# Two S4 and SwiGLU layers on one core: the convolution kernel's stage laid out by a table of times, its spread sent through DRAM, and its tail rewritten

## The chip, the cores and the metric

The kernel runs on one core of a Trainium2 chip. The metric is the device time in microseconds (us) of one launch. The engines are TensorE (PE in the profile; PEld is its weight load), VectorE (DVE), ScalarE (ACT), GpSimd (POOL) and SyncE (SP, which here only issues DMAs). Each engine works through its own list of instructions in order and waits on semaphores; DMAs are issued from SP's list and from POOL's.

## The reference, cut to what matters

```python
def _A_ref(u, ...):                       # S4 convolution, 512 channels, 128 states, L = 2048
    dt = jnp.exp(log_dt)[:, None]
    P = jnp.exp((dt * A)[:, :, None] * l)                 # channel, state, lag
    K = jnp.einsum("dn,dnl,dn->dl", C, P, dt * B).real    # the kernel of the convolution
    y = causal_convolution(u, K)                          # written there with FFTs of 4096
    return y + u * Dskip

def _B_ref(x, w_gate, w_up, w_down):      # 512 -> 1376 -> 512
    return (silu(x @ w_gate) * (x @ w_up)) @ w_down

for layer in range(2):                    # x is 2048 x 512, the same weights in both layers
    x = x + _A_ref(layernorm(x), ...)
    x = x + _B_ref(layernorm(x), ...)
```

## The kernel before, in words

Time is cut into 4 blocks of 512 rows, the channels into 8 **chunks** of 64 (`NCH`). There are four stretches.

**Start.** Inputs and tables are loaded, `dt` is formed, the factors of chunk 0 are made, and the spectra of the first input block are taken (`direct`, PE).

**Kernel stage.** One turn of a loop for each chunk i, with `K` as the product of two factors: lag = 64 b + a. Factor `g` (32 values of b, real and imaginary, 64 channels) is grown by doubling: `gen_g` (DVE) multiplies the n values it has by z^n and appends them, for n = 1, 2, 4, 8, 16. Factor `re`, `im` (64 values of a) is a cosine or sine times an exponential: `gen_turns` multiplies the angle by its table (DVE), `gen_reduce` takes off whole turns (ACT, DVE), `gen_trig` and `gen_exp` look up sine and exponentials (ACT), and `gen_e` multiplies them (DVE); `mu` holds the exponentials of the upper half. `lags` makes K with 128 small matmuls into `pk`, ACT copies it to `ks`, and `spread` moves it from rows of channel groups to rows of lags with 16 matmuls against the identity and 4 for `Dskip` (`kp`, copied to `kt`). `spectra` takes the spectra of the four blocks of K with 32 f32 matmuls of 256 columns (`pw`, four frequency groups q); ACT copies each to `s1`, POOL copies the first block into `w0r` (L503) and makes the sums of neighbouring blocks (L509), and SP stores them to `wdr` in DRAM. In a turn i, the matmuls `lags(i)` stand beside the factors of chunk i+1 and the tables of chunk i+2. Two more jobs are spread over the turns: `norms` (sums of squares of the feed-forward weights: loads by SP, squares by ACT, matmuls against ones, a maximum by DVE; they give the scales of the f16 split) and `second` (spectra of the second input block, one q a turn).

**Tail.** The last two chunks' spectra, the convolution of block 0 in layer 0 (`ssm(0, 0)`: products on DVE, inverse transform `pi` on PE), the norm of its first 256 rows, and the beginning of the split of the weights into an f16 high and low part.

**Feed-forward stretch.** For the eight pairs of layer and block: three f16 matmuls for each weight tile (high by high, high by low, low by high, L806 to L808), SiLU and product (L811 to L814), `py` (L820 to L822), with the convolution of the next pair between them.

In the first three stretches the lists of ACT, DVE and PE are in the order of the code (`manual_schedule`). That order is written out by hand with generators: `take(gg, 1)` emits the next piece of a generator. SP's and POOL's lists, and everything in the feed-forward stretch, are put in order by the scheduler. PSUM is two buffers of 4 KB a partition (`big`: `pk`, `kp`, `pgu`, `py`) and four of 2 KB (`sml`). The pieces of the code on which the change turns:

```python
def stats(...):   # G is GpSimd, V is VectorE
    G.tensor_scalar(rs[:, :rows], mv[:, :rows, 1], EPS, 1.0 / scale ** 2, OP.add, OP.mult)
    G.tensor_tensor(rs[:, :rows], rs[:, :rows], mhalf[:, :rows], OP.pow)
    G.tensor_tensor(nb[:, :rows], mv[:, :rows, 0], rs[:, :rows], OP.mult)
    G.tensor_scalar(nb[:, :rows], nb[:, :rows], -1.0, None, OP.mult)
# spectra, for each q after the copy of pw to s1:
    G.tensor_copy(w0r[:, h, q, :, off:off + DC]..., s1[:, :, 0])          # L503
    for i in range(2):
        G.tensor_tensor(wo[:, i], s1[:, i, 1:], s1[:, 1 - i, :3], ops[i])   # L509
# gen_g, the last doubling, twice 8 values of b:
    V.tensor_tensor(tmp, g[:, ::-1, b0:b0 + step], zi..., OP.mult)          # L441
    V.tensor_tensor(g[:, 0, o], g[:, 0, o], tmp[:, 0], OP.subtract)         # L444
    V.tensor_tensor(g[:, 1, o], g[:, 1, o], tmp[:, 1], OP.add)              # L445
```

Of the kernel before, what the change touches and what calls it, by code (L numbers as in the profile page):

```python
# [40 lines left out]
INV = 1  # L41
SEQ = ((0, 0), (0, 1), (0, 2), (1, 0), (0, 3), (1, 1), (1, 2), (1, 3))
# [30 lines left out]
def kernel(ctx, tc, x, a_re, a_im, b_re, b_im, c_re, c_im, log_dt, d_skip,  # L73
# [9 lines left out]
    BUFS = dict(W0=1, W1=1, W2=1, W3=1, ga=1, gb=1, n=1, bt=1, z=1, u=2, y1=1, uu=3, w=3, t=1, bb=2, dd=2, t1=3,  # L83
                xf=1, nn=1, hh=1, hl=1, sg=2, hf=1, stats=2, stats2=2, ef=1)
# [29 lines left out]
    cr, ci = load(c_re, "cr", "sg"), load(c_im, "ci", "sg")  # L114
# [20 lines left out]
    ones = tl([P, P], "ones", "dd")  # L135
    G.memset(ones, 1.0)
    onesb = sb.tile([P, P], BF16, name="onesb")
    G.memset(onesb, 1.0)
    hpi = sb.tile([P, 1], F32, name="hpi")
# [4 lines left out]
    xdr = dram.tile([NB, 4, P, D], F32, name="xdr")  # L144
    ndr = dram.tile([2, 2, P, 2, HD], F32, name="ndr")
# [34 lines left out]
    nc.sync.dma_start(dsk, d_skip)  # L180


    def stats(src, rows, scale, tag="stats", between=None):
# [10 lines left out]
        G.tensor_scalar(rs[:, :rows], mv[:, :rows, 1], EPS, 1.0 / scale ** 2, OP.add, OP.mult)  # L194
        G.tensor_tensor(rs[:, :rows], rs[:, :rows], mhalf[:, :rows], OP.pow)
        G.tensor_tensor(nb[:, :rows], mv[:, :rows, 0], rs[:, :rows], OP.mult)
        G.tensor_scalar(nb[:, :rows], nb[:, :rows], -1.0, None, OP.mult)
# [84 lines left out]
    def second(h, q, space=psml):  # L282
        n = []
        for cp in range(2):
            t = tl([P, 2, HD], "n1", "w")
            nc.sync.dma_start(t, ndr[h, cp])
            n += [t[:, 0], t[:, 1]]
        return direct(1, h, q, n, space)


    def norms():
# [7 lines left out]
        for gi, group in enumerate(groups):  # L299
            acc = psml([P, group[0][1].shape[1]], "nrm")  # L300
            for k, (wi, src) in enumerate(group):
                rows, cols = src.shape
                st = tl([P, cols], "st", "w")
                nc.sync.dma_start(st[:rows], src)
                sq = tl([P, cols], "sq", "t1", BF16)
                A.activation(sq[:rows], st[:rows], AF.Square)
                last = k == len(group) - 1

                def product(acc=acc, sq=sq, rows=rows, k=k, last=last):
                    PE.matmul(acc, lhsT=onesb[:rows], rhs=sq[:rows], start=k == 0, stop=last)  # L310
# [3 lines left out]
                yield product, largest if last else None  # L314
# [24 lines left out]
    def gen_tiles(ch):  # L339
# [3 lines left out]
        xz = tl([P, 5, DC], "xr", "bb"), tl([P, 5, DC], "xi", "dd")  # L343
# [4 lines left out]
    def gen_turns(ch, ts):  # L348

        re, im, mu, xz, mz, t16 = ts  # L350
        t_ = th[:, ch * DC:(ch + 1) * DC]
        V.tensor_tensor(t16, am[:, 5:].unsqueeze(2).to_broadcast([P, 16, DC]), bd(t_, 16), OP.mult)
        yield
        V.tensor_tensor(xz[1], am[:, :5].unsqueeze(2).to_broadcast([P, 5, DC]), bd(t_, 5), OP.mult)
        G.memset(im[:, 32], 0.0)
        yield

    def gen_reduce(ts):
# [3 lines left out]
        A.activation(xz[0].bitcast(I32), xz[1], AF.Copy)  # L362
# [8 lines left out]
        V.tensor_tensor(xz[1], xz[1], xz[0].bitcast(I32), OP.subtract)  # L371
# [14 lines left out]
    def gen_exp(ch, ts):  # L386

        re, im, mu, xz, mz, t16 = ts
# [5 lines left out]
        for a0, o in ((0, re), (32, mu)):  # L394
            for a in [a for a in range(a0 + 1, a0 + 33) if a < 64 and (a % 2 or a % 8 == 0)]:
                A.activation(o[:, a - a0], r_, AF.Exp, scale=32.0 * a)
                yield
            for st in (2, 4):
                A.activation(o[:, st:33:2 * st] if a0 == 0 else o[:, st::2 * st],
                             re[:, (a0 + st) // 2:(a0 + 34) // 2:st], AF.Square)  # L400
                yield

    def gen_e(ts):


        half = [[t.rearrange("p a (g h d) -> p a g h d", g=4, h=2)[:, :, :, o] for t in ts[:3]] for o in range(2)]
# [6 lines left out]
        for re, im, mu in half:  # L413
            V.tensor_tensor(re[:, 33:64], re[:, 33:64], mu[:, 1:], OP.mult)
            yield
            V.scalar_tensor_tensor(im[:, 33:64], im[:, 33:64], -1.0, mu[:, 1:], OP.mult, OP.mult)
            yield

    def gen_g(ch, ts, g):
# [12 lines left out]
        for n in (1, 2, 4, 8, 16):  # L432
            yield
            lv = n.bit_length() - 1
            zr, zi = (t[:, lv:lv + 1, :].unsqueeze(1) for t in xz)
            V.tensor_tensor(g[:, :, n:2 * n], g[:, :, 0:n], zr.to_broadcast([P, 2, n, DC]), OP.mult)
            step = min(n, 8)
            for b0 in range(0, n, step):
                tmp = tl([P, 2, 8, DC], "tmp", "bt")[:, :, :step]
                o = slice(n + b0, n + b0 + step)  # L440
                V.tensor_tensor(tmp, g[:, ::-1, b0:b0 + step], zi.to_broadcast([P, 2, step, DC]), OP.mult)  # L441
                if b0 + step == n:
                    yield
                V.tensor_tensor(g[:, 0, o], g[:, 0, o], tmp[:, 0], OP.subtract)  # L444
                V.tensor_tensor(g[:, 1, o], g[:, 1, o], tmp[:, 1], OP.add)  # L445
        yield

    def lags(ts, g):
        re, im = ts[:2]
        pk = pbig([P, 16, 64], "pk")  # L450
        for d in range(DC):
            grp, dd = d % 4, d // 4
            d = 16 * grp + dd
# [391 lines left out]
    with tc.manual_schedule(engines={mybir.EngineType.Activation, mybir.EngineType.DVE, mybir.EngineType.PE}):  # L845
# [171 lines left out]
        while tops:  # L1017
            tops.pop(0)()
# [76 lines left out]
```

## Time and profile before

| | |
|---|---|
| device time, median of 3 runs | 1219.86 us (1213.67 to 1221.53) |
| device time of the profiled execution | 1211.11 us |
| span of the profiled execution | 1209.3 us |
| start (to the first `lags`) | 54.3 us |
| kernel stage, `lags` of chunk 0 to `lags` of chunk 7 | 235.6 us |
| tail, `lags` of chunk 7 to the first feed-forward matmul | 59.7 us |
| feed-forward stretch | 859.7 us |
| busy PE, DVE, ACT, POOL | 1129.1, 1041.4, 632.1, 191.7 us |

The stretches are the stages of one profiled execution, cut where `lags` begins (54.3, 289.9) and where the first matmul of the feed-forward stretch begins (349.6). "Busy" is the time in which an engine had an instruction running. A row of the timeline has its start, its length, the engine, line and operation, output and inputs, the size, how many are merged in it, and in brackets the idle time before it and what ended it. Instructions overlap a little, so the step from one start to the next is shorter than the length shown. One f32 matmul of the code stands as two MATMUL rows.

### The profile page before, as it was taken

How to read it: one execution, taken by the hardware profiler on the slowest of the kernel's cores; microseconds unless marked ns; L12 is line 12 of the kernel's file. 1: busy time of each engine (PE TensorE's matmuls, PEld its weight loads, DVE VectorE, ACT ScalarE, POOL GpSimd, SP SyncE). 2: the span in 40 equal slices, each digit the busy share in tenths (PEclk: the TensorE clock that was granted, in tenths of full speed). 3: DMA queues.
4: the chain of work that ended last, by engine and by line, in shares of the span. 5: the costliest groups of instructions: out<-in, count | busy, mean ns of one | idle time of the engine just before them, and what ended most of it. 6: DMA issues, size and time to landing. Idle time of an engine off the chain costs nothing.

```text
span 1209.3 us, 25387 instructions
## 1 busy us (share of the span) xinstructions
PE 1129.1 (93%) x10220; PEld 887.6 (73%) x10220; DVE 1041.4 (86%) x1685; ACT 632.1 (52%) x1392; POOL 191.7 (16%) x209
## 2 busy tenths in 40 slices
PE   3989999979988998989999999999999999999998
PEld 2867878767876686858686877777686776867875
DVE  7999999988769999899999999999993799983221
ACT  6998888852256445536754623564432553324111
POOL 1024437653130010101100000120000010000000
PEclk9999999989999999999999999999999999999999
DMA  6223322236389425632245453334434144311000
GB/s 227 105 86 89 86 72 70 83 94 179 108 258 312 123 71 169 160 118 90 69 135 148 128 169 133 110 96 146 141 118 138 37 116 132 117 58 44 14 23 18
DMA packets 134857, 138.66 MB, mean 115 GB/s; under 512 B 75921, under 2 KB 85137, under 8 KB 134738
## 3 DMA queue, kind: packets, MB, share of 16 engines
q1 hardware_dynamic: 132178, 128.64, 35.4%
q0 software_dynamic: 2560, 8.39, 2.0%
q8 instruction: 80, 1.31, 0.5%
q14 instruction: 39, 0.32, 0.1%
HBM read 98.71 MB, written 28.31 MB: 105 GB/s over the span
## 4 chain that ended last, share of the span: by engine, by line
PE 34%; DVE 25%; issue 5%; DMA 3%; ACT 2%; POOL 2%; SPq 1%; DVEq 0%; ACTq 0%; POOLq 0%
PE pgu L806 6%; PE pgu L807 6%; PE pgu L808 6%; DVE t L682 4%; PE py L820 4%; PE py L821 3%; PE py L822 3%; DVE yk L685 3%; PE pi L701 3%; PE pf L260 2%; DVE yk L682 2%; DVE z L216 2%; POOL rs L211 2%; DMA mix<-nn 2%; DVE sg L812 1%
## 5 line engine op out<-in xcount | busy, mean ns | idle before, releaser
L806 PE MATMUL pgu<-mix,wsl 128*128 128x256 f16 x1280 | 349.6, 273 | 6.4 <-DVE sg L812 3.8
L808 PE MATMUL pgu<-mix,wsl 128*128 128x256 f16 x1280 | 349.7, 273 | 1.3 <-DVE wsl L578 1.3
L807 PE MATMUL pgu<-mix,wsl 128*128 128x256 f16 x1280 | 349.7, 273 | 0.0
L807 PEld LDWEIGHTS <-wsl 128*128 128x128 f16 x1280 | 125.5, 98 | 22.9 <-issue 7.2
L820 PE MATMUL py<-wsl,hh 128*128 128x512 f16 (+1 forms) x352 | 134.5, 382 | 7.6 <-DVE xg L825 3.5
L808 PEld LDWEIGHTS <-wsl 128*128 128x128 f16 x1280 | 125.5, 98 | 16.6 <-DVE wsl L578 1.6
L806 PEld LDWEIGHTS <-wsl 128*128 128x128 f16 x1280 | 125.5, 98 | 15.7
L822 PE MATMUL py<-wsl,hl 128*128 128x512 f16 (+1 forms) x352 | 134.4, 382 | 2.4 <-DVE hl L814 2.4
L811 ACT ACTIVATE sg<-pgu,sc 128x512 f32<-128x512 f32 x80 | 54.6, 682 | 132.0 <-PE pgu L808 114.1
L682 DVE TENSOR_TENSOR t<-uu,w 128x1024 f32<-128x1024 f32 x96 | 118.1, 1230 | 5.6 <-DMA uu<-udr 5.4
L821 PE MATMUL py<-wsl,hh 128*128 128x512 f16 x320 | 122.1, 382 | 0.0
L685 DVE TENSOR_TENSOR yk<-yk,t 128x1024 f32<-128x1024 f32 x96 | 118.0, 1229 | 0.2
L812 DVE SCALAR_TENSOR_TENSOR sg<-pgu,sc,sg 128x512 f32<-128x512 f32 x80 | 60.4, 756 | 52.2 <-ACT sg L811 52.0
L492 PE MATMUL pw<-kt,ek 128*128 128x256 f32 (+2 forms) x420 | 103.1, 386 | 0.0
L701 PE MATMUL pi<-yl,mix 128*128 128x256 f16 x672 | 91.4, 272 | 4.1 <-ACT yl L690 3.5
L492 PEld LDWEIGHTS pw<-kt,ek 128*128 128x128 f32 x420 | 81.9, 203 | 10.9
L813 ACT ACTIVATE hh<-sg 128x512 f16<-128x512 f32 x80 | 50.0, 625 | 57.8 <-DVE sg L812 57.7
L503 POOL COPY w0r<-s 128x128 f32<-128x128 f32 x29 | 58.5, 2016 | 127.1 <-ACT s L501 98.4
L211 POOL TENSOR_TENSOR rs<-mv,mhalf 128x2 f32<-128x2 f32 (+1 forms) x21 | 36.5, 1740 | 263.8 <-ACT mv L210 248.3
L260 PE MATMUL pf<-z,eh 128*128 128x256 f16 x576 | 74.6, 273 | 1.3 <-ACT z L250 1.3
L701 PEld LDWEIGHTS <-mix 128*128 128x128 f16 x672 | 65.3, 98 | 13.3 <-issue 2.4
L682 DVE TENSOR_TENSOR yk<-u,w0r 128x1024 f32<-128x1024 f32 x56 | 68.7, 1227 | 0.3 <-ACT u L262 0.3
(221 smaller groups left out, 2336.3 us busy)
## 6 DMA issues: line engine op xcount, KB each, us to landing
w<-wdr SPq DMA_DIRECT2D x96, 256.0 KB, 2.8
uu<-udr SPq DMA_DIRECT2D x96, 256.0 KB, 3.0
udr<-u POOLq DMA_DIRECT2D x32, 256.0 KB, 2.7
wdr<-wo SPq DMA_DIRECT2D x96, 64.0 KB, 2.0
udr<-u SPq DMA_DIRECT2D x16, 256.0 KB, 2.5
n<-ndr SPq DMA_DIRECT2D x16, 256.0 KB, 2.9
n<-xdr SPq DMA_DIRECT2D x4, 1024.0 KB, 5.5
xg<-in_A_u_dram SPq DMA_DIRECT2D x3, 1024.0 KB, 6.1
```

Of the source, the lines that this page charges most:

```text
L260: PE.matmul(pf[:, o], lhsT=e, rhs=m, start=k == 0, stop=k == len(terms) - 1)
L492: PE.matmul(pw[:, i], lhsT=e, rhs=kt[:, :, c + 4 * k0:4 * k1:4, :].rearrange("p g k d -> p k g d"), start=c == 0, stop=c == 3)
L682: V.tensor_tensor(t, uu.unsqueeze(1).to_broadcast([P, 2, 2, HD]), w.unsqueeze(2).to_broadcast([P, 2, 2, HD]), OP.mult)
L685: V.tensor_tensor(yk, yk, t, OP.add)
L701: PE.matmul(pi[:, o], lhsT=e, rhs=m, start=k == 0, stop=k == len(terms) - 1)
L806: PE.matmul(o, lhsT=wgu(wi, k, 0)[:, fs], rhs=nh[:, k], start=k == 0, stop=False)
L807: PE.matmul(o, lhsT=wgu(wi, k, 0)[:, fs], rhs=nlo[:, k], start=False, stop=False)
L808: PE.matmul(o, lhsT=wgu(wi, k, 1)[:, fs], rhs=nh[:, k], start=False, stop=k == 3)
L812: V.scalar_tensor_tensor(sg, pgu[:, 1], sc6[:, 4:5], sg, OP.mult, OP.mult)
L820: PE.matmul(py[:, r], lhsT=hh[:n, f, rc], rhs=wd(f, 0)[:n], start=f == 0, stop=False)
L821: PE.matmul(py[:, r], lhsT=hh[:n, f, rc], rhs=wd(f, 1)[:n], start=False, stop=False)
L822: PE.matmul(py[:, r], lhsT=hl[:n, f, rc], rhs=wd(f, 0)[:n], start=False, stop=f == FT - 1)
```

## The change

- **Order.** The turns of the kernel stage and the tail are no longer written as a sequence of `take`. Every piece is entered in a list with a time (`at(t, piece)`), the list is sorted, and the pieces are emitted in that order. SP's list in this stretch is in the order of the code now. The times only set the order.
- **g.** The subtraction and the addition of a doubling become one addition for both parts, with the negative sine made by ACT (`xz[:, 2]`). The last doubling of chunks 1 to 7 makes its second product in one instruction, and a DMA from POOL's queue adds it to `g` (`accum_op=OP.add`).
- **mu.** The upper half's exponentials are squares of the lower half's: one ACT instruction (`upper`) for 19 exponentials and 2 squares. For chunks 6 and 7 the angles are made by ACT in 21 small instructions, not by DVE.
- **Spread.** For chunks 0 to 5 `kt` is made by a DMA to DRAM (`kdr`) and four back. Chunks 6 and 7 use the identity matmuls. `Dskip` is added in `products` by a matmul of one row.
- **Spectra.** Two q at a time into one `big` buffer; ACT makes the signed copy from PSUM and `w0r`, DVE adds (L552 of the new code), and SP stores with one DMA for each q.
- **norms.** The loads go to POOL's queue, and loads, squares, products and maxima have times of their own.
- **stats.** The small operations around the power go from POOL to DVE.
- **Tail.** `spectra_parts` in place of `spectra`; the convolution is cut into two halves (`ssm_half`) whose pieces have times; the norm of the first rows is a generator (`first_norm`); the split of the weights uses other buffers in another order.
- **Feed-forward stretch.** The four low-by-high matmuls come after the eight others of a group; one tile `sg2` with two halves replaces two buffers of `sg`.

```diff
 def stats(src, rows, scale, tag="stats", between=None, then=None):
...
-    G.tensor_scalar(rs[:, :rows], mv[:, :rows, 1], EPS, 1.0 / scale ** 2, OP.add, OP.mult)
+    V.tensor_scalar(rs[:, :rows], mv[:, :rows, 1], EPS, 1.0 / scale ** 2, OP.add, OP.mult)
     G.tensor_tensor(rs[:, :rows], rs[:, :rows], mhalf[:, :rows], OP.pow)
-    G.tensor_tensor(nb[:, :rows], mv[:, :rows, 0], rs[:, :rows], OP.mult)
-    G.tensor_scalar(nb[:, :rows], nb[:, :rows], -1.0, None, OP.mult)
+    if then:
+        then()
+    V.scalar_tensor_tensor(nb[:, :rows], mv[:, :rows, 0], -1.0, rs[:, :rows], OP.mult, OP.mult)
...
+def upper(ts):
+    A.activation(ts[2][:, 1:], ts[0][:, 1:32], AF.Square)
...
+        if n == 16 and ch:
+            tmp = tl([P, 2, 16, DC], "acc", ("gb", "ga")[ch % 2] if ch < NCH - 1 else "W0")
+            V.tensor_tensor(tmp, g[:, ::-1, 0:16], xz[:, 2:0:-1, lv:lv + 1].to_broadcast([P, 2, 16, DC]), OP.mult)
+            G.dma_start(g[:, :, 16:32].rearrange("p i b d -> p i (b d)"), tmp.rearrange("p i b d -> p i (b d)"),
+                        accum_op=OP.add)
+            continue
...
+def spread(ch, ks, kt, eng=nc.sync):
+    k = kdr[ch % 2]
...
+    eng.dma_start(k.rearrange("g b a f -> (g b) a f"), ks.rearrange("p a c d -> p a (c d)"))
+    for ga in range(4):
+        eng.dma_start(kt[32 * ga:32 * ga + 32].rearrange("p g c d -> p g (c d)"), k[:, :, ga].rearrange("g b f -> b g f"))
...
+def spectra(ch, kt, q0):
...
+    pw = pbig([P, 2, 2, NB, 4, 16], "pw")
+    for j in range(2):
+        products(ch, pw[:, j], kt, 0, NB, q0 + 2 * j, [(i, c) for i in range(2) for c in range(4)])
+    yield
...
+    for i, sign in signs(q0):
+        A.activation(wv[:, :, i], pv[:, :, 1 - i, :3 * DC], AF.Copy, scale=sign)
+    A.activation(w0r[:, h, q0::2, :, off:off + DC], wf[:, :, :, 0], AF.Copy)
+    yield
+    V.tensor_tensor(wv, pv[:, :, :, DC:], wv, OP.add)
+    yield
+    for j in range(2):
+        store_w(h, off, q0 + 2 * j, wo[:, j])
...
+    def use(c, t):
...
+        at(t, lambda: box.update(pk=lags(ts[c], gs[c])))
+        at(t + 7.1, copy)
...
+    starts = [0.0, 31.0, 62.0] + [93.0 + 28.0 * k for k in range(NCH)]
+    for i in range(NCH - 1):
+        t = starts[i]
+        use(i, t)
+        factors(i + 1, t)
+        second_block(i, t)
+        if i + 2 < NCH:
+            prepare(i + 2, t)
...
                     for k in range(4):
                         PE.matmul(o, lhsT=wgu(wi, k, 0)[:, fs], rhs=nh[:, k], start=k == 0, stop=False)
-                        PE.matmul(o, lhsT=wgu(wi, k, 0)[:, fs], rhs=nlo[:, k], start=False, stop=False)
-                        PE.matmul(o, lhsT=wgu(wi, k, 1)[:, fs], rhs=nh[:, k], start=False, stop=k == 3)
+                        PE.matmul(o, lhsT=wgu(wi, k, 1)[:, fs], rhs=nh[:, k], start=False, stop=False)
+                    for k in range(4):
+                        PE.matmul(o, lhsT=wgu(wi, k, 0)[:, fs], rhs=nlo[:, k], start=False, stop=k == 3)
```

Three places of the engines' lists follow. First DVE's list from the last doubling of `g` to the start of the next turn, in a turn of the kernel stage. `acc` and `tmp` hold the second product, `spare` and `wo` are the sums for `wdr`. Before:

```order
L436 TENSOR_TENSOR g<-g,xr 128x2x1024
L441 TENSOR_TENSOR tmp<-g,xi 128x1024
L444 TENSOR_TENSOR g<-g,tmp 128x512
L445 TENSOR_TENSOR g<-g,tmp 128x512
L441 TENSOR_TENSOR tmp<-g,xi 128x1024
L414 TENSOR_TENSOR re<-re,mu 128x124x8
L416 SCALAR_TENSOR_TENSOR im<-im,mu 128x124x8
L444 TENSOR_TENSOR g<-g,tmp 128x512
L445 TENSOR_TENSOR g<-g,tmp 128x512
```

And now:

```order
L469 TENSOR_TENSOR g<-g,xz 128x2x1024
L472 TENSOR_TENSOR acc<-g,xz 128x2048
L552 TENSOR_TENSOR spare<-pw,spare 128x768
L393 TENSOR_TENSOR xz<-xz 128x320
L396 SCALAR_TENSOR_TENSOR im<-t_1237,re 128x1024
L396 SCALAR_TENSOR_TENSOR im<-t_1237,re 128x512
L396 SCALAR_TENSOR_TENSOR im<-t_1237,re 128x256
L396 SCALAR_TENSOR_TENSOR im<-t_1237,re 128x128
L396 SCALAR_TENSOR_TENSOR im<-t_1237,re 128x64 x2
L443 TENSOR_TENSOR re<-re 128x32x32 x2
L446 TENSOR_TENSOR re<-re,mu 128x31x32
L448 SCALAR_TENSOR_TENSOR im<-im,mu 128x31x32
```

The four additions of 512 are gone, a sum over 768 elements of `pw` has come in behind `acc`, and the taking off of whole turns (L393, L396), which stood between the doublings, now follows it. Second, POOL's list in one turn of the kernel stage (`s` is the copy of `pw`; the two memsets belong to the tables of a later chunk). Before:

```order
L503 COPY w0r<-s_1021 128x2x64
L509 TENSOR_TENSOR wo<-s_1021 128x192 x2
L393 MEMSET re 128x64
L355 MEMSET im 128x64
L503 COPY w0r<-s_1095 128x2x64
L509 TENSOR_TENSOR wo<-s_1095 128x192 x2
```

And now:

```order
L473 DMA g<-acc 128x2x1024
L418 MEMSET re 128x64
L377 MEMSET im 128x64
L316 DMA st<-in_B_w_gate_dram 128x344 x3
L473 DMA g<-acc 128x2x1024
```

POOL's arithmetic on `s` is gone from the stage; the adding DMA and the loads of weights have taken its place. Third, DVE's list in the start, at the mean and variance of the first input block (`mv`, `rs`). Before:

```order
L192 BN_STATS st<-xne 128x6
L193 BN_AGGR mv<-st 128x2
L371 TENSOR_TENSOR xi<-xi,xr 128x320
L374 SCALAR_TENSOR_TENSOR im<-t_163,re 128x1024
L374 SCALAR_TENSOR_TENSOR im<-t_163,re 128x512
```

And now:

```order
L203 BN_STATS st<-xne 128x6
L204 BN_AGGR mv<-st 128x2
L205 TENSOR_SCALAR rs<-mv 128x4
L209 SCALAR_TENSOR_TENSOR rs<-mv,rs 128x4
L393 TENSOR_TENSOR xz<-xz 128x320
L396 SCALAR_TENSOR_TENSOR im<-t_166,re 128x1024
```

Two small instructions have come in; the second reads what POOL's power makes of the first's result, and the rest of DVE's list stands behind it. The same pair stands again behind the statistics of the second block.

More of the change, by code (lines that the diff above doesn't have):

```diff
@@ L134 @@
     G.memset(epst[:, 1:2], EPS / 256.0 ** 2)
[L135 removed]
+    ones = tl([P, P], "ones", "bd")
     G.memset(ones, 1.0)
@@ L138 @@
     G.memset(onesb, 1.0)
+    one = sb.tile([P, 1], F32, name="one")
+    G.memset(one, 1.0)
     hpi = sb.tile([P, 1], F32, name="hpi")
```

641 lines of the change are left out of this document (345 added, 296 removed).

## The prediction, made before the result was known

> **What bounds the kernel now.** I read the busy shares of the stages first, cut at DVE's turns of the kernel stage and at the starts of `lags`. The columns are length, then busy PE, PEld, DVE, ACT, POOL with counts, then granted clock and DMA.
>
> ```profile
> 58.87:89.68 30.81, 26.84 (x310) 21.00 (x304) 30.74 (x48) 29.98 (x89) 6.49 (x8) 0.94 0.29 90
> 89.68:123.39 33.71, 32.30 (x383) 25.72 (x375) 33.64 (x49) 30.57 (x88) 16.26 (x15) 0.95 0.32 87
> ...
> 220.80:261.70 40.90, 32.65 (x383) 26.18 (x382) 37.32 (x57) 30.57 (x91) 25.52 (x17) 0.87 0.29 77
> 261.70:289.90 28.20, 26.80 (x372) 21.99 (x372) 26.58 (x32) 10.68 (x28) 13.10 (x10) 1.00 0.50 147
> 289.90:349.60 59.70, 55.94 (x531) 49.52 (x531) 45.01 (x89) 18.82 (x30) 18.47 (x28) 0.97 0.54 160
> 349.60:1209.30 859.70, 825.29 (x6913) 636.12 (x6911) 719.11 (x1176) 378.26 (x717) 57.99 (x70) 0.99 0.38 115
> ```
>
> A turn is DVE's: 33.64 busy in 33.71 us. The first turn, with 6.5 us of POOL instead of 16, is 2.9 us shorter for nearly the same list. The tail and the feed-forward stretch are PE's (55.9 of 59.7; 825 of 860). In the stage 220.80 to 261.70 all engines idle; the waits name a late load of weights:
>
> ```profile
> ACT sq L306 <- DMA st<-in_B_w_up_dram: 7.1, 1, 7.1
> ```
>
> Next, whether DVE's work is slow or much. Equal instructions in the start (rows 1, 3) and in the stage (rows 2, 4), where POOL's copies and sums run, mean ns after the comma:
>
> ```profile
> L416 DVE SCALAR_TENSOR_TENSOR im<-im,mu 128x992 f32<-128x992 f32 x2 | 2.4, 1189 | 0.0
> L416 DVE SCALAR_TENSOR_TENSOR im<-im,mu 128x992 f32<-128x992 f32 x10 | 13.9, 1387 | 0.0
> ...
> L352 DVE TENSOR_TENSOR t<-am,th 128x1024 f32<-128x1024 f32 x1 | 1.2, 1222 | 0.0
> L352 DVE TENSOR_TENSOR t<-am,th 128x1024 f32<-128x1024 f32 x5 | 8.0, 1599 | 0.0
> ...
> L503 POOL COPY w0r<-s 128x128 f32<-128x128 f32 x17 | 33.8, 1988 | 63.1 <-ACT s L501 34.4 <-DMA st<-in_B_w_gate_dram 28.6
> L509 POOL TENSOR_TENSOR wo<-s 128x192 f32<-128x192 f32 x32 | 31.6, 1007 | 0.0
> ```
>
> DVE is 17 to 31% slower there.
>
> **The sum, against the profiled execution's 1211.1 us.**
>
> *DVE's turn.* Undisturbed steps from start to start:
>
> ```profile
> 42.23 1.22 DVE L441 TENSOR_TENSOR tmp<-g,xi 128x1024 f32<-128x1024 f32 x1
> 43.36 0.42 DVE L374 SCALAR_TENSOR_TENSOR im<-t,re 128x256 f32<-128x256 f32 x1
> 43.70 0.69 DVE L444 TENSOR_TENSOR g<-g,tmp 128x512 f32<-128x512 f32 x1
> ...
> 45.37 2.29 DVE L436 TENSOR_TENSOR g<-g,xr 128x2048 f32<-128x2048 f32 x1
> 47.57 1.22 DVE L441 TENSOR_TENSOR tmp<-g,xi 128x1024 f32<-128x1024 f32 x1
> ```
>
> 1.13 for 1024, 0.34 for 256, 2.20 for 2048: 0.07 us and N/960 us for N elements. A turn before is 46 instructions of 24,704 elements: 3.2 + 25.7 = 29.0 us undisturbed, so POOL's neighbourhood costs 4 to 5. Afterwards it is 38 instructions of 24,512 elements, 28.2 us: the last doubling's four sums leave (2048 elements), two sums of `pw` come in (1536). DVE's own saving is only 0.8; the gain is the disturbance, and POOL's arithmetic on SBUF is gone.
>
> *The chain that takes its place.* `lags`, then ACT up to its signed copies of `pw`, then DVE's sum (L552) and what stands behind it up to the first half of `gen_e`, which frees the next `lags`. ACT's steps:
>
> ```profile
> 130.38 1.02 ACT L461 ACTIVATE ks<-pk 128x1024 f32<-128x1024 f32 x1 [4.05 <-PE pk L456]
> 131.30 0.46 ACT L362 ACTIVATE xr<-xi 128x320 int32<-128x320 f32 x1
> 131.66 2.37 ACT L368 ACTIVATE re<-t 128x1024 int32<-128x1024 f32 x6
> ...
> 144.92 1.28 ACT L391 ACT_TABLE_LOAD   x1
> ...
> 147.55 1.24 ACT L306 ACTIVATE sq<-st 128x344 bf16<-128x344 f32 x3
> ...
> 149.75 1.85 ACT L396 ACTIVATE re<-rho 128x64 f32<-128x64 f32 x12
> 151.50 1.07 ACT L399 ACTIVATE re<-re 128x512 f32<-128x512 f32 x2
> ```
>
> 0.9 + 1.1 + 0.4 + 2.3 + 1.3 + 25 exponentials at 0.15 (3.7) + 1.0 + copies 0.8 = 11.5. With `lags` 8.4 (row below) and DVE's 0.87 + 0.40 + 2.54 + 2.27 + 2.20 = 8.3, the chain is 28.2 long, level with DVE. The mu squares cost ACT 1.8 for 4 us, at nothing, since ACT has idle time; so do the 21 angle copies of chunks 6 and 7 (3.1), which lie before `ks`.
>
> *PE's turn.*
>
> ```profile
> 239.73 0.59 PE L492 MATMUL pw<-kt,ef 128*128 128x256 f32 x2
> 240.16 1.46 PE L492 MATMUL pw<-kt,ek 128*128 128x256 f32 x6
> 241.46 0.59 PE L492 MATMUL pw<-kt,ef 128*128 128x256 f32 x2
> ...
> 121.80:152.50 30.70, 8.41 (x256) 8.14 (x256) 1.02 (x1) 1.00 0.30 83
> ...
> 214.68 1.07 PE L310 MATMUL nrm<-sq,onesb 128*128 128x344 bf16 x3 [1.50 <-ACT sq L306]
> 216.35 2.77 PE L492 MATMUL pw<-kt,ek 128*128 128x256 f32 x6
> ```
>
> Four products take 1.73, so 32 take 13.8; with `lags` 8.4, `Dskip` rows 0.6, `second` 3.5 and the ones 1.2 it is 27.5. After 1.5 us without work the same six rows take 2.77 instead of 1.46 and the granted clock of such turns is 0.95: about 1.7 us lost. PE would wait 1 us a turn, so I add it: 29.2. The Trainium skill ("TensorE: Matmul & The Clock Gate", What's actually happening) says that the clock halves after an idle window of some 3.4 us; this trace differs, since 1.5 us were enough. By that rule the turns would be 0.8 us shorter and the sum 4 us less. The new order of columns in `products` reads with a stride; the strided reads of `lags` (64 columns a row, 8.41/256 = 33 ns) are faster per column than `pw` needs, so I cost it at nothing; a halved rate would be +13.8 a turn.
>
> *The adding DMA.* It is issued behind DVE's `acc`, 17.7 us into the turn (24 instructions, 15,360 elements), and `lags` reads its result; with turns of 29.5 the room is 10.6 us. No such DMA is in the trace. Nearest rows:
>
> ```profile
> udr<-u POOLq DMA_DIRECT2D x32, 256.0 KB, 2.7
> n<-xdr SPq DMA_DIRECT2D x4, 1024.0 KB, 5.5
> st<-in_B_w_down_dram SPq DMA_DIRECT2D x2, 1024.0 KB, 8.2
> ```
>
> It moves 1 MB and also reads its target: 5.5 at least, 16 at most (8.2 twice). I take 8, from the two 1 MB rows, so nothing waits. The skill's page "DMA: Bandwidth & Descriptors" (Anatomy of one DMA, SWDGE) gives 2.0 us and bytes/436e3, an estimate of 4.4 us; no run here shows an accumulating one. Behind it in POOL's list stand loads of weights, each freed by a square on ACT. *Spread through DRAM:* three steps of 2 to 3 us and four issues, some 7 us; PE has `pw` of the last chunk, the ones and `second` (12 us) to do meanwhile. If that cover went, at most 2 us a turn.
>
> *The stage:* 28 for the first turn (no `pw` of an earlier chunk), 29.5 for five, and for the last PE's 8.4 + 14.4 + 2.6 + 3.5 + 1.8 and a little wait, 31.5: 207 against 235.6 (54.3 to 289.9). **-28.6**, of which 11 are the late load.
>
> *Start.* DVE is without idle time there, and twice it now waits for POOL's power:
>
> ```profile
> 15.58 1.88 POOL L195 TENSOR_TENSOR rs<-rs,mhalf 128x4 f32<-128x4 f32 x1
> ...
> 31.00 1.90 POOL L195 TENSOR_TENSOR rs<-rs,mhalf 128x4 f32<-128x4 f32 x1
> ```
>
> With two small instructions each 2.2: **+4.4**.
>
> *Tail, PE again.*
>
> ```profile
> 316.58 1.50 PE L492 MATMUL pw<-kt,ek 128*128 128x64 f32 x12
> ...
> 330.14 1.14 PE L492 MATMUL pw<-kt,ek 128*128 128x192 f32 x6
> 331.12 0.59 PE L276 MATMUL pf<-n,ef 128*128 128x256 f32 x2
> ...
> 340.65 1.36 PE L747 MATMUL pt<-ident,nn 128*128 128x128 f32 x8 [3.32 <-ACT nn L745]
> ```
>
> A product of 64 columns costs 0.25, of 192 0.33 (three, six rows, from 330.14 to 331.12). Afterwards: `lags` 8.9, 32 `pi` 13.8, `kp` 2.6, 48 short ones 12.0, `Dskip` 0.8, 32 of 192 10.4, 8 `pf` 3.5, `pt` 1.4: 53.4 and 1.6 of waits, 55. **-4.7**. But 16 products of 192 now come behind the first feed-forward group: +5.2, partly in that stretch's idle time (34 us). The nlo matmuls are as many as before; I cost their order at nothing, within 8 us either way. **+3**.
>
> Sum: 1211.1 + 4.4 - 28.6 - 4.7 + 3 = 1185. The median shown lies 8.75 above the profiled time; I go half of that way: **1189**.
>
> **The rivals.**
> - *Everything closes up.* No clock drops, turns of 28, fewer waits late: 5 x -1.5 and -8, 1169 by the profiled time. For it: DVE, chain and PE are all below 28.3. Against it: three engines level seldom run without waits.
> - *The adding DMA is late by some us, and the kernel still faster.* If it takes D, `lags` is late by the excess, `ks` and L552 too, but not the `acc` ahead of L552; so half lands on a turn: 24.2 + D/2. D of 12 to 16 gives 30.2 to 32.2: 1189 to 1199 by the profiled time.
> - *The adding DMA is so late that it is slower.* Same place; the stage's gain is gone at turns of 35.2 (D of 22), and at D of 27 a turn of 37.7 makes 1211 + 4.4 + 12.4 - 1.7 = 1226. Beyond my bound of 16, but possible with the loads ahead of it in POOL's list.
> - *It doesn't do what it says.* DVE is slow for another reason (ACT, DMA writes): 28.2 + 4.6 = 32.8 a turn, five times +3.3: 1201 by the profiled time. Against it: the first turn.
>
> **Chances.** Forecast 0.62, closing up 0.10, late but faster 0.12, slower 0.05, no relief 0.11. A time within 1% of the median (1208 to 1232) is about what a measurement of this kernel can't tell from no change. The forecast lies 19 us below that, no relief and late partly in it: faster 0.85, same 0.11, slower 0.04. The range reaches from closing up to no relief: 1168 to 1210.
>
> **What would show it.** Right: DVE's `L448` and `L368` back at 1.19 and 1.22 us, POOL nearly idle in the stage, `lags` to `lags` 29 to 30 us, first `lags` at 58 to 59, first feed-forward matmul near 321, no 7 us wait for a load. Wrong: `lags` waiting for the DMA into `g`; L552 waiting several us for ACT; PE at half clock for more than 3.4 us a turn; `pw` rows above 1.46.

## The result, and the profile after

| | before | after |
|---|---|---|
| device time, median | 1219.48 us (1213.67 to 1221.53) | 1324.3 us (1320.73 to 1329.73) |
| span of the profiled execution | 1209.3 us | 1320.8 us |
| start | 54.3 us | 58.1 us |
| kernel stage (`lags` 0 to `lags` 7) | 235.6 us | 319.1 us |
| tail | 59.7 us | 76.7 us |
| feed-forward stretch | 859.7 us | 867.0 us |

The ratio is 1.087 (95% interval 1.082 to 1.093): the changed kernel is slower by 8.7%, where 1189 us was forecast. 83 of the 111 us by which the spans differ lie in the kernel stage, 17 in the tail. The busy times by stage of the changed kernel, in the columns of the prediction's first fence (length, then busy PE, PEld, DVE, ACT, POOL with counts, granted clock, DMA):

```profile
58.07:96.34 38.27, 33.76 (x314) 23.31 (x314) 37.65 (x44) 31.60 (x64) 4.83 (x9) 0.87 0.53 144
96.34:143.44 47.10, 47.10 (x352) 28.87 (x351) 33.92 (x40) 35.33 (x63) 4.75 (x9) 1.00 0.41 104
143.44:189.60 46.16, 46.16 (x351) 28.40 (x350) 33.21 (x38) 32.99 (x63) 4.85 (x9) 1.00 0.41 104
...
377.15:453.81 76.66, 76.66 (x549) 63.18 (x549) 48.96 (x80) 20.29 (x37) 1.34 (x1) 0.87 0.37 111
453.81:1320.84 867.03, 837.36 (x6946) 643.42 (x6944) 725.87 (x1200) 382.95 (x734) 53.09 (x69) 0.99 0.38 114
```

A turn is PE's from end to end, 47.10 busy in 47.10 us, at full clock. The second row of the prediction's fence (89.68 to 123.39) had 32.30 with 383 matmul rows; here are fewer rows and half as much time again. POOL is down to 5 us, as forecast. So the bound moved to PE, and PE's instructions became longer, not more. Which ones, PE's timeline in one turn shows (start, length, line, size, rows merged):

```profile
156.33 2.87 PE L522 MATMUL pw<-kt,ek 128*128 128x256 f32 x6
159.03 1.05 PE L522 MATMUL pw<-kt,ef 128*128 128x256 f32 x2
159.90 2.81 PE L522 MATMUL pw<-kt,ek 128*128 128x256 f32 x6
...
170.08 0.62 PE L325 MATMUL nrm<-sq,onesb 128*128 128x344 bf16 x3
170.53 0.59 PE L288 MATMUL pf<-n,ef 128*128 128x256 f32 x2
170.96 1.46 PE L288 MATMUL pf<-n,ek 128*128 128x256 f32 x6
```

The trace holds its own control: `pf` and `pw` have the same shape, type and weights. `pf` reads 256 neighbouring values and six rows take 1.46 us; `pw` reads `kt` in the new order and six rows take 2.8. `lags` is longer too. PE's windows over two of its executions (busy PE, clock, DMA):

```profile
143.40:155.00 11.60, 11.60 (x258) 1.00 0.01 3
189.60:202.10 12.50, 12.50 (x258) 1.00 0.01 3
```

Before, the same 256 rows took 8.41 us. And what ACT and DVE do beside `lags` (143.4 to 155.0) takes far longer than the same thing elsewhere in the same turn; idle time ahead of an instruction stands in brackets:

```profile
143.54 2.77 ACT L549 ACTIVATE wo<-pw 128x384 f32<-128x384 f32 x2 [4.77 <-PE pw L522]
146.69 6.00 ACT L426 ACTIVATE mu<-re 128x1984 f32<-128x1984 f32 x1
170.29 0.87 ACT L549 ACTIVATE spare<-pw 128x384 f32<-128x384 f32 x2 [4.32 <-PE pw L522]
...
146.94 3.65 DVE L552 TENSOR_TENSOR wo<-pw,wo 128x768 f32<-128x768 f32 x1 [6.66 <-ACT w0r L550]
171.47 0.96 DVE L552 TENSOR_TENSOR spare<-pw,spare 128x768 f32<-128x768 f32 x1 [5.78 <-ACT w0r L550]
```

The signed copies take 2.77 instead of 0.87, the sum 3.65 instead of 0.96. Both effects point at one edit that is spread over two lines. `lags` used to take channel `16 * grp + dd` (that line is gone), so the four column groups that run side by side read channels 16 apart. Now it takes `4 * dd + grp`, four neighbours. To bring the channels back into their order, `products` reads `kt` as block, channel, group: four columns that stand 1 KB apart, then the next four, where it was 16 neighbours at a time.

### The profile page after: what moved, and what is told of

Its sections match the earlier page's. It is cut to its first block, busy times and chain, and to the rows that moved or that the text cites. A ratio compares the mean times of both kernels' runs of the same rounds, so it can differ in the third digit from the quotient of the medians.

```text
span 1320.8 us, 24840 instructions
## 1 busy us (share of the span) xinstructions
PE 1260.5 (95%) x10076; PEld 929.8 (70%) x10076; DVE 1048.6 (79%) x1631; ACT 670.5 (51%) x1310; POOL 92.1 (7%) x152
## 4 chain that ended last, share of the span: by engine, by line
PE 52%; DVE 34%; issue 7%; DMA 3%; ACT 2%; POOL 1%; SPq 1%; DVEq 0%; ACTq 0%; POOLq 0%
PE pw L522 18%; DVE t L761 5%; DVE yk L764 4%; PE pk L493 4%; PE pgu L893 4%; PE pgu L894 4%; PE pgu L896 4%; PE pk L492 3%; DVE yk L761 3%; PE py L908 3%; DVE z L228 3%; PE py L909 3%; PE py L910 3%; PE pi L780 2%; DMA mix<-nn 2%
## 5 line engine op out<-in xcount | busy, mean ns | idle before, releaser
L893 PE MATMUL pgu<-mix,wsl 128*128 128x256 f16 x1280 | 301.0, 274 | 5.7 <-DVE sg L900 4.4
L894 PE MATMUL pgu<-mix,wsl 128*128 128x256 f16 x1280 | 300.9, 274 | 1.4 <-DVE wsl L655 1.4
L896 PE MATMUL pgu<-mix,wsl 128*128 128x256 f16 x1280 | 196.9, 274 | 0.0
L522 PE MATMUL pw<-kt,ek 128*128 128x256 f32 (+2 forms) x456 | 187.6, 563 | 0.0
L522 PEld LDWEIGHTS pw<-kt,ek 128*128 128x128 f32 x456 | 90.6, 219 | 69.7 <-issue 58.6
L900 DVE SCALAR_TENSOR_TENSOR sg<-pgu,sc,sg 128x512 f32<-128x512 f32 x80 | 59.5, 744 | 53.9 <-ACT sg L899 53.7
L492 PE MATMUL pk<-re,g 128*32 128x64 f32 x1024 | 88.4, 363 | 3.5 <-DVE g L483 3.5
L493 PE MATMUL pk<-im,g 128*32 128x64 f32 x1024 | 88.9, 361 | 0.0
L492 PEld LDWEIGHTS pk<-re,g 128*32 128x32 f32 x1024 | 69.0, 164 | 10.2 <-issue 8.8
```

The costliest lines, as they stand in the source:

```text
L492: PE.matmul(o, lhsT=g[:, 0, :, d], rhs=re[:, 0:64, d], start=True, stop=False, tile_position=(0, 32 * grp))
L493: PE.matmul(o, lhsT=g[:, 1, :, d], rhs=im[:, 0:64, d], start=False, stop=True, tile_position=(0, 32 * grp))
L522: PE.matmul(pw[:, i], lhsT=e, rhs=kt[:, :, c + 4 * k0:4 * k1:4, :].rearrange("p g k d -> p k d g"), start=c == 0, stop=c == 3)
L893: PE.matmul(o, lhsT=wgu(wi, k, 0)[:, fs], rhs=nh[:, k], start=k == 0, stop=False)
L894: PE.matmul(o, lhsT=wgu(wi, k, 1)[:, fs], rhs=nh[:, k], start=False, stop=False)
L896: PE.matmul(o, lhsT=wgu(wi, k, 0)[:, fs], rhs=nlo[:, k], start=False, stop=k == 3)
```

## The experiments

**Undo the assignment of channels, whole and in halves.** Both lines put back in the changed kernel (`e1_both_back`), only the columns of `products` (`e2_products_back`), only `lags` (`e3_lags_back`), and the new assignment put alone into the kernel before (`e4_before_new`):

```diff
 # lags
             grp, dd = d % 4, d // 4
+            d = 16 * grp + dd
 # products
-            PE.matmul(..., rhs=kt[:, :, c + 4 * k0:4 * k1:4, :].rearrange("p g k d -> p k d g"), ...)
+            PE.matmul(..., rhs=kt[:, :, c + 4 * k0:4 * k1:4, :].rearrange("p g k d -> p k g d"), ...)
```

> The changed kernel with the old assignment of channels: in lags channel 16*grp+dd again instead of 4*dd+grp, and in products the columns again in the order block, group, channel (16 neighbours in SBUF) instead of block, channel, group (each column 1 KB from the one before). Theory A (the assignment of channels is the cause: the strided columns double every product with 256 or 192 columns, and four neighbouring channels side by side make lags 3 to 4 us longer): pw rows back to 1.46 for six, lags back to 8.4 us, turns 29 to 32 us instead of 46 to 47, first feed-forward matmul at 320 to 335, time 1185 to 1210 us. Rival B (PE is slowed by its neighbours, the adding DMA, the spread through DRAM and ACT's additional work on SBUF, whatever the columns): rows of 2.8 and turns of 45 us stay, 1310 to 1330 us.

> The changed kernel with the old order of columns in products alone; lags keeps the new assignment, so the channels of the convolution's kernel come out in another order. Theory A: pw rows at 1.46 for six, lags still 11 to 12.5 us, and ACT and DVE still two to three times slower beside lags; turns of 31 to 34 us, time 1210 to 1240 us. Rival C (only the columns matter; lags is longer because PE is late and runs against other work than before): lags falls to 8.4 to 9 us too, time as with both parts put back, 1185 to 1210 us.

> The changed kernel with the old assignment in lags alone; products keeps its strided columns, so the channels come out in another order. Theory A: lags back to 8.4 us, pw rows stay at 2.8 for six, DVE's sum of pw beside lags back from 3.0 to about 1 us; turns of 42 to 44 us, 8 times 3 to 4 us less than the changed kernel: 1290 to 1305 us. Rival C: lags stays at 11 to 12 us and the time at 1315 to 1330 us.

> The kernel before with nothing but the new assignment of channels, in lags, in products and in the rows of Dskip. Theory A: pw rows 2.8 for six, lags 11 to 12.5 us, turns of 46 to 50 us instead of 33.6, time 1310 to 1345 us, as slow as the changed kernel or slower. Rival B: 1215 to 1235 us.

| | time, us | turns 2 to 6, us | first feed-forward matmul |
|---|---|---|---|
| before | 1214.99 | 30.7 to 40.9 | 349.6 |
| after (first comparison) | 1324.3 | 45.6 to 47.1 | 453.8 |
| `e1_both_back` | 1204.68, ratio 0.991 (0.987 to 0.995) | 29.7 to 33.2 | 340.0 |
| `e2_products_back` | 1242.52 (one run) | 33.7 to 40.7 | 378.1 |
| `e3_lags_back` | 1301.27 (one run) | 42.9 to 43.4 | 430.5 |
| `e4_before_new` | 1325.57 (one run) | 47.1 to 51.1 | 467.1 |

Theory A's mechanism holds in all four: those two lines are 120 us of 1324, and put alone into the kernel before they cost it 111 us. Rivals B and C fall. Some of its bounds were too narrow: in `e1` the first feed-forward matmul comes at 340.0 instead of 320 to 335, with turns up to 33.2 instead of 32; in `e2` turns reach 40.7 instead of 34 and the time is 2.5 us above the bound; in `e4` turns reach 51.1 instead of 50, and `lags` takes 14.35 in the turn of 49.9. Against `e1`, the new columns of `products` alone cost 97 us (`e3`) and the new `lags` alone 38 (`e2`), each in one run. The halves, from the windows of `lags` and of a turn in `e2_products_back`:

```profile
200.75:211.85 11.10, 11.10 (x256) 1.00 0.13 46
...
165.42:200.75 35.33, 32.50 (x349) 27.42 (x350) 35.05 (x40) 33.87 (x64) 4.17 (x8) 1.00 0.58 149
```

and in `e3_lags_back`:

```profile
183.16:191.50 8.34, 8.34 (x257) 1.00 0.02 4
...
183.16:226.06 42.90, 42.90 (x350) 25.40 (x349) 28.19 (x37) 26.72 (x62) 4.21 (x8) 1.00 0.43 107
```

With the columns put back alone, `lags` stays at 11.1 us and DVE fills the turn (35.05 of 35.33, ACT 33.87; nearly the same lists take 28.19 and 26.72 in the other half): the neighbours of `lags` pay more than `lags`. With `lags` put back alone, it is 8.34 again, and the turn of 42.9 is PE's with long `pw`.

**How far apart, and for whom.** `e11_steps` (1256.61 us, one run; only its rows are read) gives each chunk another step between the columns of `products`, and another distance between the four channels of `lags`:

```diff
+            d = dd // sep * 4 * sep + grp * sep + dd % sep       # sep = 16, 1, 2, 4, 8, 16, 16
...
+            step = (1, 2, 4, 16, 64, 0, 0, 0)[ch]
+            if step:
+                cols = kt[:, c].rearrange("p k d -> p (k d)").rearrange("p (n e) -> p e n", e=step)
```

> e5_pool_order with another order of columns in the products of each chunk of the stage and another distance of the four channels that stand side by side in lags, to measure both alone; the numbers of the convolution's kernel come out in another order, so only the times of these rows are read. Products read 256 values that stand 4, 8, 16, 64 and 256 bytes apart in chunks 0 to 4, and the changed kernel's order (1024 bytes apart, four at a time) in chunk 5; lags takes channels 16, 1, 2, 4, 8, 16 apart (64, 4, 8, 16, 32, 64 bytes) in chunks 0 to 5. Theory A1 (any step but 4 bytes halves PE's reading): 1.46 us for six rows in chunk 0, 2.8 in all others. Theory A2 (only steps of 64 bytes or more do): 1.46 to 8 or 16 bytes, 2.8 from 64 on. For lags, theory L1 (four channels in one stretch of 64 bytes collide): 11 to 12.5 us for distances of 1, 2, 4 and 8, 8.4 for 16. Theory L2 (the nearer the worse): a length that falls step by step from 12 to 8.4.

Six rows of `pw`, in chunks 0 to 5 (4, 8, 16, 64, 256, 1024 bytes):

```profile
106.63 1.46 PE L530 MATMUL pw<-kt,ek 128*128 128x256 f32 x6
...
120.83 1.52 PE L530 MATMUL pw<-kt,ek 128*128 128x256 f32 x6
...
154.51 2.88 PE L530 MATMUL pw<-kt,ek 128*128 128x256 f32 x6
...
196.91 2.76 PE L530 MATMUL pw<-kt,ek 128*128 128x256 f32 x6
...
239.37 2.82 PE L530 MATMUL pw<-kt,ek 128*128 128x256 f32 x6
...
282.47 2.81 PE L530 MATMUL pw<-kt,ek 128*128 128x256 f32 x6
```

Neither A1 nor A2: a step of 8 bytes costs 4%, from 16 bytes on everything costs about twice (2.76 to 2.88), and further apart is no worse. The Trainium skill states this ("SBUF — State Buffer", Door 1: The DMA port swizzle): SBUF has lines of 16 bytes, and full bandwidth takes at least two hits in a line. The trace agrees: 1.52 us at 8 bytes, where two f32 stand in a line, and 2.88 at 16, where one does. I hadn't weighed that rule in the prediction, and it speaks straight against the change. Now `lags`, at distances of 4, 8, 16, 32 and 64 bytes (chunks 1 to 5):

```profile
91.30:103.80 12.50, 12.50 (x257) 1.00 0.01 3
126.50:136.00 9.50, 9.50 (x258) 1.00 0.37 114
165.00:172.30 7.30, 7.30 (x257) 1.00 0.02 4
207.00:215.30 8.30, 8.30 (x257) 1.00 0.01 4
249.70:258.00 8.30, 8.30 (x257) 1.00 0.11 25
```

Neither L1 nor L2: 4 bytes is the worst, 16 bytes the best, better than the 64 of before. ACT's squares of 1984 elements beside them, at 4 and at 16 bytes:

```profile
95.80 8.19 ACT L426 ACTIVATE mu<-re 128x1984 f32<-128x1984 f32 x1
...
166.21 1.91 ACT L426 ACTIVATE mu<-re 128x1984 f32<-128x1984 f32 x1
```

**What was left of the forecast.** `e1_both_back` is 20 us above my sum of 1185. Its stage is 221.6 instead of 207, its tail 59.5 instead of 55. The longest overrun is the first turn's, 33.1 instead of 28. There PE waits 3.93 us for a square on ACT at the matmul of ones, and the `pw` rows behind it run at half clock:

```profile
79.55 1.62 PE L325 MATMUL nrm<-sq,onesb 128*128 128x512 bf16 x3 [3.93 <-ACT sq L322]
...
82.57 2.93 PE L523 MATMUL pw<-kt,ek 128*128 128x256 f32 x6
```

Of the later turns two are long (31.7 and 33.2), and the chain of work that ended last shows by what:

```profile
113.64 0.54 POOL st L316
114.17 9.37 DMA g<-acc
123.67 0.49 PE pk L493 x3
```

The adding DMA takes 9 us, close to the 8 of the sum, but POOL issues it behind a load that waits for ACT. `e5_pool_order` puts POOL's list in the order of the table, `e8_dve_adds` does without the DMA, `e6_exps_late` moves the exponentials behind the copies of `pw`, and `e7_tail_mix` puts longer products between the tail's short ones:

```diff
 # e5: twice
-        with tc.manual_schedule(engines={mybir.EngineType.SP}):
+        with tc.manual_schedule(engines={mybir.EngineType.SP, mybir.EngineType.Pool}):
 # e6, on e5
-            at(t + 12.6, steps["exp"], 100)
+            at(t + 14.05, steps["exp"], 100)
 # e7, on e1 (and the later at() of odd taken out)
-        at(t + 11.0, start, 8)
+        at(t + 10.5, odd, 2); at(t + 11.0, start, 4); at(t + 11.1, odd)
+        at(t + 11.2, odd, 2); at(t + 11.3, start, 4); at(t + 11.4, odd)
 # e8, on e1
-        if n == 16 and ch:
+        if n == 16 and ch > NCH:
```

> e1_both_back with POOL's list in the order of the table too, so that the adding DMA stands ahead of the third group of weight loads. In e1 the DMA is issued at 114.2 and 176.8 us behind a load that waits for a square on ACT, and lags starts at its landing, in the turns of 31.7 and 33.2 us. Theory A (what is left of the stage's loss is the late issue of the adding DMA): these two turns 29.5 to 30.5 us, stage 215 to 218 us instead of 221.6, time 1198 to 1202 us. Rival B (the DMA's own 9 us or the chain over ACT sets the turns anyway): turns of 31 to 32, 1203 to 1206 us.

> e1_both_back with the last doubling's second product added by DVE (two products and two additions of 1024) instead of by the adding DMA. Theory A (the DMA's issue and 9 us of landing set two turns; DVE has idle time): lags never waits for g, turns of 30 to 31.5 us, 1200 to 1204 us. Rival B (DVE is the bound, so its 2.3 us a turn show): turns longer by 2 us, 1212 to 1218 us.

> e5_pool_order with the exponentials of a turn behind ACT's copies of pw instead of ahead of them (one number of the table). Theory A (DVE's sum of pw waits 16 us in all for copies that stand behind 5.6 us of exponentials, and the factors of the next lags stand behind that sum): that wait falls to under 5 us, turns go to PE's own 29.4 us, stage 209 to 214 us, 3 to 5 us less than e5. Rival B (PE's work of 29.4 to 30 us already sets the turns): the wait goes and the time stays within 2 us of e5.

> e1_both_back with the tail's short products (64 columns) no longer six groups in a row (19 us in e1, of which the last 13.6 at a granted clock of 0.50, without any idle time of PE): two groups of 192 columns stand between them. Theory A (a row of short products over more than about 7 us halves the clock): no stretch at 0.50 in the tail, 52 to 54 us from the last lags to the first feed-forward matmul beside the 59.5 of e1, counting that four groups of 192 columns still stand behind it as in e1. Rival B (the clock falls for another reason, a DMA-less stretch or the matmuls of one row for Dskip): 0.50 is granted again for 13 us.

`e5_pool_order`: 1201.77 us (0.987, 0.983 to 0.991); the two turns fall to 30.7 and 30.2, `lags` no longer waits for the DMA, and the stage is 216.8. Theory A by these rows; the times alone don't part it from `e1` (0.991, 0.987 to 0.995). Only part of the stage's 4.8 us is the DMA's: the two turns give 4.0, two others lose 2.1, and 3.0 come from the first turn (30.1 now), where the wait for ACT is 2.25 us and is followed by full clock. `e8_dve_adds`: 1204.67 us (0.990, 0.986 to 0.994), turns of 31.5 to 32.5, longer than Theory A's, at a time far from Rival B's. As fast as `e1`: the adding DMA, which looks like the change's strongest idea, is worth nothing over two additions of 1024 on DVE as long as it is issued late. Issued in time it is worth some 0.8 us a turn by the stages of one execution each (216.8 in `e5`, 222.1 here); the times of `e5` and `e8` don't part them.

`e6_exps_late`: 1228.95 us (1.010, 1.006 to 1.015), a plain miss. DVE's wait for the copies only moved: ahead of `spare` it fell from 12.3 to 5.7 us in all, and 10.7 came ahead of `wo`. Besides, this came:

```profile
PE nrm L325 <- ACT sq L322: 18.8, 5, 3.8
ACT spare L550 <- PE pw L523: 16.2, 5, 3.3
```

ACT now idles some 3 us for `pw` before it starts the exponentials, so its squares of the weights come later, and PE stands at the matmul of ones behind them. Turns 2 to 6 are 35.3 to 37.2 us, and the clock granted in windows of a turn's length there is 0.90 to 0.94. The exponentials had been filling ACT's wait.

`e7_tail_mix` (1215.3 us, one run): the half clock stays, `pi`, moved back, adds waits, and the tail is 75.9 us instead of the 52 to 54 of Theory A. In `e1` and `e7` PE is busy all the time, and yet:

```profile
306.00:308.00 2.00, 2.00 (x12) 0.50 0.00 0
308.00:310.00 2.00, 2.00 (x9) 0.50 0.01 4
```

(`e1`), and in `e7`, 3.6 us after the first short product:

```profile
300.00:304.00 4.00, 4.00 (x20) 0.60 0.00 0
304.00:308.00 4.00, 4.00 (x15) 0.55 0.00 0
```

So it doesn't take six groups in a row. Before, there were no matmuls of one row (`Dskip`) among them. `e10_dskip` takes these out for chunks 6 and 7, and `e12_start_angles` also undoes two parts of the change that I had priced:

```diff
 # e10, on e5: in products, and in spread_pe as in the kernel before
-            if (i, c) == (0, 0) and k0 == 0:
+            if (i, c) == (0, 0) and k0 == 0 and ch < NCH - 2:
...
+            PE.matmul(kp[0:32, grp, 0], lhsT=ident[0:1, 0:32], rhs=dsk[:, d0:d0 + 16], start=False, stop=True, ...)
 # e12, on e10: stats of the start on POOL again, and in gen_turns
-        if ch < 6:
+        if ch < NCH:
```

> e5_pool_order with Dskip added for chunks 6 and 7 as in the kernel before (one matmul of 16 columns for each group of channels into kp) instead of the matmul of one row beside every product. In e7 the clock still fell to 0.50, 3.6 us after the first short product; the kernel before has 5.3 us of short products without one-row matmuls among them and keeps 1.00. Theory A (short products halve the clock only with the one-row matmuls among them): no stretch at 0.50 in the tail, which is 59.5 - 6.8 - 1.4 = 51 to 53 us; time 1191 to 1196 us. Rival B (short products do it by themselves when there are more than three groups): the half clock stays, the tail is 57 to 59 us, time 1199 to 1202 us.

> e10_dskip with the small operations around the power in the start back on POOL, as in the kernel before, and the angles of chunks 6 and 7 back on DVE. Theory A (DVE's two waits for the power cost the start 4.4 us; the 21 angle copies lengthen ACT's chain in the two turns of 31.6 and 30.8 us): first lags at 54 to 55 us instead of 59, these turns 30 to 31 us, 4 to 7 us less than e10: 1186 to 1192 us. Rival B (the start's end is set by another wait that takes the place, ACT's or a load's): first lags at 57 to 59 us and within 2 us of e10.

PE over the short products of `e10`, and the feed-forward stretch behind them:

```profile
293.40:304.10 10.70, 10.70 (x98) 1.00 0.00 1
...
326.20:1201.00 874.80, 836.11 (x6947) 643.08 (x6944) 729.98 (x1206) 384.49 (x734) 59.12 (x69) 0.98 0.38 115
```

Theory A: full clock over all six groups, with no DMA beside them, and a tail of 51.2 us. But the time is 1203.01 us (0.990, 0.986 to 0.993), no better than `e5`: the feed-forward stretch is 12.5 us longer (862.3 in `e5`), with 38.7 us without a matmul instead of 31.3. Its list is the scheduler's. In the traces, ACT's instructions of this stretch come in one and the same order in the changed kernel and in nine of its versions, `e5` and `e12` among them; in `e10` the same instructions come in another order. Why the scheduler made it, and which wait in it costs the 12 us, stays open. `e12` has the usual list again:

```profile
326.37:1188.10 861.73, 830.98 (x6946) 641.62 (x6944) 729.42 (x1205) 383.30 (x734) 52.93 (x69) 0.99 0.39 117
```

`e12` runs 1190.59 us (0.979, 0.976 to 0.983), but not by what it was made for. The first `lags` starts at 55.5 instead of 58.3, the second at 88.7 instead of 88.4. In between PE, now early, waits 3.9 us for a square on ACT where `e10` has 2.2, and what follows runs at half clock for 6.8 us; `e10` has half clock too, but for 3.4 us, behind an earlier wait of 1.66. `e12`, then `e10`:

```profile
76.17 1.62 PE L331 MATMUL nrm<-sq,onesb 128*128 128x512 bf16 x3 [3.93 <-ACT sq L328]
...
79.19 2.93 PE L532 MATMUL pw<-kt,ek 128*128 128x256 f32 x6
```

```profile
78.98 1.42 PE L325 MATMUL nrm<-sq,onesb 128*128 128x512 bf16 x3 [2.24 <-ACT sq L322]
...
81.19 1.56 PE L526 MATMUL pw<-kt,ek 128*128 128x256 f32 x6
```

The two turns with the angles stay at 30.8 and 31.6. The time lies in Theory A's range, but by luck: neither theory's start came (54 to 55 or 57 to 59), other waits took its gain away, as Rival B says, and all of the 12 us against `e10` lie in the feed-forward stretch (874.8 and 861.7).

**The distance that the steps suggested.** 80 bytes is 16 more than 64, so each group may begin four channels further on within its own sixteen, and the columns stay neighbours:

```diff
-            grp, dd = d % 4, d // 4
+            grp = d % 4
+            dd = (d // 4 + 4 * grp) % 16
             d = 16 * grp + dd
```

> e12_start_angles with the four channels that stand side by side in lags 80 bytes apart instead of 64 (each group begins four channels further on within its own sixteen; the result is the same and products still read 16 neighbours). In e11_steps the rows of lags stepped 47, 36, 27.5, 32 and 32 ns at distances of 4, 8, 16, 32 and 64 bytes, and ACT's and DVE's instructions beside it took two to four times as long at 4 bytes. Theory S1 (what counts is where the four stand within 64 bytes: 16 bytes apart, as 80 is, all four read side by side): 27.5 ns, lags 7.3 us instead of 8.4, turns 0.5 to 1 us shorter, time 1181 to 1187 us. Theory S2 (the distance itself counts, and anything from 32 bytes on is alike): 32 ns, 8.4 us, time within 3 us of e12, 1188 to 1194 us.

Two turns and the tail of `e13_staggered`:

```profile
87.24:116.89 29.65, 28.89 (x352) 23.60 (x351) 25.75 (x35) 24.89 (x60) 4.82 (x9) 1.00 0.65 168
...
177.39:206.56 29.17, 28.71 (x350) 23.68 (x350) 28.27 (x39) 25.35 (x62) 4.24 (x8) 1.00 0.59 148
...
268.67:319.38 50.71, 50.63 (x546) 45.64 (x546) 37.64 (x75) 16.27 (x37) 1.34 (x1) 1.00 0.49 149
```

`lags` without waits in it is 7.4 us (87.24 to 94.65, where `e12` has 8.4), rows step 28.1 ns, turns are 0.1 to 1.6 us shorter. Theory S1 holds. The time is 1184.12 us, ratio 0.974 (0.971 to 0.978): this version is faster than both kernels, by 2.6% and by 10.6% (1184.12 of 1324.3, from two comparisons).

## Why the prediction was wrong

The step that failed is one sentence of "PE's turn": "The new order of columns in `products` reads with a stride; the strided reads of `lags` (64 columns a row, 8.41/256 = 33 ns) are faster per column than `pw` needs, so I cost it at nothing; a halved rate would be +13.8 a turn." The alternative was worked out rightly (a product takes 0.87 us from 159.03 to 159.90, where it took 0.43: 14.1 us a turn) and then left out of the range and of the rivals. The reason was misread: in `lags` four matmuls run side by side, so 33 ns is the step of four streams. One of them gets a row every 131 ns for 64 columns, 2.05 ns a column; `pw` before needed 1730 ns for eight rows of 256, 0.84 ns a column. So the row that I quoted is no ground for a cost of nothing. It doesn't show the price of a stride either: the tail's products of 64 columns read neighbours, and at 0.25 us for two rows they take 1.95 ns a column too. The stride was first measured in `e11`. With ends of 0 and 13.8 us a turn, the range had to reach 13.8 x 6 = 83 us higher. The sign that I had named, `pw` rows above 1.46 us, came; the chance of 0.04 for slower was meant for a late adding DMA and not for this.

Second, the lost line `d = 16 * grp + dd` stands neither in my account of the change nor in the sum. It made `lags` some 3 to 4 us longer and slowed ACT and DVE beside it.

The other steps, read from the runs without these two lines:

- **DVE free of POOL: right.** In `e1` the two forms that I named, in the stage (mean ns after the comma):

```profile
L448 DVE SCALAR_TENSOR_TENSOR im<-im,mu 128x992 f32<-128x992 f32 x15 | 17.7, 1181 | 0.0
...
L368 DVE TENSOR_TENSOR t<-am,th 128x1024 f32<-128x1024 f32 x4 | 4.9, 1224 | 0.0
```

- **The turn: a little low, and near only because two errors met.** 29.5 was forecast, 30.2 to 31.6 came in `e5`. The 1.7 us that I took for the clock are not there: those five turns have a granted clock of 1.00. But PE is busy for 29.7 to 30.4 instead of my 27.5, most of it in `pw` with its `Dskip` rows (16.5 instead of 14.4). The chain is longer than my 28.2, since `lags` also waits for the second half of `gen_e` (`im` of L448; 2.7 us in five times), at which I had stopped.
- **The clock: one row read as a rule.** I took 1.5 us without work as enough for half clock. In the first turn of `e5` and of `e10` a gap of 1.66 us was followed by 0.50 and one of 2.2 by 1.00, in `e12` 1.66 by 1.00 and 3.9 by 0.50. So the length of one gap doesn't settle it here.
- **The adding DMA: near in length (8 taken, 9.0 measured), wrong in its issue.** The room for it is 11.8 us by my own numbers (29.5 less 17.7), not 10.6; 9.0 fits either. The loads of weights ahead of it in POOL's list, which I named for the rival, made it late in two turns.
- **The start: right in size, wrong in effect.** The first `lags` came 3.7 us later (4.5 in `e1`); `e12` shows that the second one doesn't come sooner when this is undone, since a longer wait for ACT and a longer stretch of half clock take the gain back.
- **The tail: 55 forecast, 59.5 in `e1`.** What I had left out was the clock: 6.8 us are the loss in 13.6 us at 0.50, and `e10` without them has 51.2.
- **The feed-forward stretch: +3 forecast, +3.2 in `e1`** (862.9), and +2.0 to +3.7 in `e5`, `e6`, `e8`, `e12` and `e13`. That the size came out is luck as far as the runs show: none tests the two terms it was made of, and `e10`'s other order moves the stretch by 12.5 us.

That `e12` and `e13` land at 1190.6 and 1184.1 doesn't make the forecast right: they are other kernels.

## What to carry to other kernels

Before an access pattern is costed at nothing, find a row of the same length that reads with that step in one stream; rows that run side by side, or that are short, don't tell. When a rearrangement changes what stands beside what, ask who reads there how often: here 32 products a turn became 14 us longer, and the 128 small matmuls some 3 us. And a term whose two ends lie 83 us apart belongs in the range, whichever end looks likelier.

## What the runs showed of the hardware

- A single stream of f32 columns: 1.46 us for six rows of 256 at a step of 4 bytes, 1.52 at 8, 2.76 to 2.88 from 16 to 1024 bytes.
- Four matmuls side by side on groups of 32 columns: 12.5, 9.5, 7.3, 8.3, 8.3 us for 256 rows at distances of 4, 8, 16, 32, 64 bytes, and 7.4 at 80. At 4 bytes, ACT's and DVE's instructions beside them take two to four times as long (8.19 us for 1.91). That these meet at the same place in SBUF is my reading; the runs show the times alone.
- PE can be busy without a gap and still lose its clock: products of 64 columns with matmuls of one row among them fell to 0.50 after 3.6 us (`e7`) or 7.5 us (`e1`), the same products without them kept 1.00 for 10.7 us (`e10`). It isn't a sharp rule: a last such row in `e7`, 4.8 us long, kept 1.00. The Trainium skill ("TensorE: Matmul & The Clock Gate", What's actually happening) ties half rate to an idle window; here PE was busy in 2.00 of 2.00 us by the profile while 0.50 was granted.
